# Fixed tables for the order of calls and of engine queues, a tie maximum in PSUM, and a norm by columns, in a fused attention, Fourier and FFN kernel

## Chip, cores and metric

The kernel runs as one program on one core of a Trainium2 chip. The metric is the device time of one execution in microseconds, as the median of several runs. The core's engines each take their instructions in a fixed order: TensorE (PE, with its weight loads as PEld), VectorE (DVE), ScalarE (ACT), GpSimd (POOL) and SyncE (SP), which here only issues DMAs. Between engines the order is kept by semaphores.

## The reference

For 4 batches, 8 heads, 768 tokens and head size 64 the reference computes an attention in which a query sees only keys of its own cluster, then a block that mixes by Fourier transforms, and an FFN.

```
q_assign = argmax(q_n . c_n);  k_assign = argmax(k_n . c_n)      # 16 centroids per head
scores = where(q_assign == k_assign, q k^T / 8, -1e9);  x = softmax(scores) v      # x: 4 x 768 x 512
mixed = real(fft(fft(x, axis=1), axis=2));  u = x + mixed
un = (u - mean(u)) / sqrt(var(u) + 1e-6)
out = u + relu(un @ w_ch1) @ w_ch2                                # 512 -> 2048 -> 512
```

All of it is to fp32 accuracy. The kernel gets there with products of fp16 halves: a value is scaled by a power of two and split into a high and a low half, and three products (high by high, high by low, low by high) are summed in PSUM.

## The kernel before, in words

Two heads make a pair; there are 16 pairs, 4 to a batch.

`prep(pr)` loads q and k of a pair (one buffer, tag `scr`), takes their largest values and that of v (L492, L524), makes scales, splits q and k into halves (L511, L512), multiplies by the centroids (L539, one PSUM tile `ps_f`), transposes the products into a second `ps_f` tile (L547) and finds the cluster of each token: the maximum over 16 centroids (L553), an equality (L555), a product with tie weights on POOL (L557), the maximum of that (L561, to an SBUF tile `mx`), and three equalities with that maximum (L565 for q, L569 twice for k). The one-hot result is transposed by a DMA.

`scores(pr, st)` makes, for one of six blocks of 128 queries, the score tiles of both heads: 12 matmuls on 64 rows (L596) and 4 mask matmuls on 32 rows (L601) into tiles `ps_big`. Here that is called a score group. For each head follow a scaled maximum on DVE (L615), Exp on ACT (L618), a cast to the high half on ACT (L626), the low half on POOL (L627) and a transposing DMA (L629). `attend` multiplies by v: 18 matmuls for a head and block (L647 to L649), called a product. After each third block `finish` divides by the sums (L659 to L663) into X. `load_v` loads v of a pair; a one-element copy on POOL (L465) from the latest score maximum into the tile ahead of the load ties it to that moment.

`Weights` brings the 32 pieces of the two FFN matrices in through 8 buffers in a scratch region (`arena`) and turns them into fp16 halves: sign bits on ACT (L782, L783), a block maximum (L767, L770), a join (L791, L795) and the halving (L801 to L807).

For a batch whose four pairs are through, `Fourier` folds X (L918, L919), splits and transposes it, and runs the two transforms as matmuls (L977, L993). `FeedForward.norm` gets mean and variance of two tiles of 128 tokens (L1083, L1084), then a power of two near the inverse deviation by five operations on two columns at once (L1085, L1086, L1088, L1090, L1091), applies it on ACT (L1094), splits and transposes. `up` makes 16 hidden blocks of 12 matmuls (L1127, an up group), each with a Relu to fp32 (L1132 or L1134), one to fp16 (L1135) and a difference (L1136); `down` has 8 groups of 12 matmuls (L1157) and two outputs (L1161). A batch has three such blocks of 256 tokens.

PSUM tiles come from three pools: `ps_f` with 3 banks (prep, weights, transforms, FFN), `ps_big` with 2 tiles, `ps_o` with 1.

What runs when is set in two steps. `Overlap.run` gives every call a step of a schedule by constants (T0, STEPS, V, WD, MIX and others), and fills FFN work in by credits; that is the order of the program. `Order` then takes the list of instructions, gives each a cost and its dependencies, plays the engines through in the kernel's own planner (`schedule`) and ties each engine's instructions together in the order that came out:

```
order, self.end = self.schedule()
for xs in order.values():
    for a, b in zip(xs, xs[1:]):
        self.tc.add_manual_dep(self.L[b], self.L[a].name, ...)
```

Of the kernel before, what the change touches and what calls it, by code (L numbers as in the profile page):

```python
# [13 lines left out]
F32 = mybir.dt.float32  # L14
# [42 lines left out]
def top_power(nc, tops, t, s, inv):  # L57

    t = t.bitcast(I32)
    nc.vector.tensor_scalar(out=t, in0=tops.bitcast(I32), scalar1=23, scalar2=None, op0=ALU.logical_shift_right)  # L60
    nc.vector.tensor_scalar(out=t, in0=t, scalar1=-13.0, scalar2=1.0, op0=ALU.add, op1=ALU.max)
    nc.vector.tensor_scalar(out=inv.bitcast(I32), in0=t, scalar1=240.0, scalar2=float(1 << 23), op0=ALU.min, op1=ALU.mult)
    nc.vector.reciprocal(out=s, in_=inv)
# [13 lines left out]
class Order:  # L77
# [6 lines left out]
    LINEAR = {"DVE": (135, 1.0), "Activation": (105, 0.92), "Pool": (160, 1.15)}  # L84
    SMALL = {"DVE": 75, "Pool": 100}
    TWO = {"DVE": 1.17, "Pool": 1.9}
    EXTRA = (
        (lambda e, i, acc: e == "DVE" and len([a for a in acc if a[1]]) > 1, 110),
        (lambda e, i, acc: e == "DVE" and any(a[1] and a[0].startswith("oh_") for a in acc), 310),
        (lambda e, i, acc: e == "Activation" and i.opcode == "TensorCopy", -75),  # L90
        (lambda e, i, acc: e == "Pool" and "pow" in str(getattr(i, "op", "")), 500),
    )
    AFTER = {"DVE": 75, "Activation": 100, "Pool": 40, "PE": 160}
    WAKE = {"DVE": 35, "Activation": 35, "Pool": 78, "PE": 52, "SP": 27}
    COPY, TURN, LAND, RATE = (530, 2150), (960, 0.46), 1790, (0.32, 0.65)
    STRETCH, TURNED = 3413.0, 80
    LATER = ()

    def __init__(self, tc, pools):
        self.tc, self.nc, self.bufs, self.cuts = tc, tc.nc, pools, []  # L100
        self.first = len(self.traced())
# [4 lines left out]
    def cut(self, stream):  # L106
        self.cuts.append((len(self.traced()) - self.first, stream))

    @staticmethod
    def base(name):  # L110
        return name.rstrip("0123456789").rstrip("_")

    def accesses(self, i):

        for w, side in ((0, i.ins), (1, i.outs)):
            for a in side:
                t = getattr(getattr(a, "bass_ap", None), "tensor", None)
                if t is None:
                    continue
                es = {F32: 4, I32: 4, U32: 4, F16: 2, BF16: 2, I16: 2, U16: 2}.get(a.dtype, 4)  # L120
                ap, off = [list(x) for x in a.ap], a.bass_ap.offset
                row = ap[0][0] or 1
                lo = hi = off % row
                n = 1
                for s, c in ap[1:]:
                    n *= c
                    lo, hi = (lo, hi + s * (c - 1)) if s >= 0 else (lo + s * (c - 1), hi)
                yield t.name, w, (off // row, off // row + ap[0][1], lo * es, (hi + 1) * es), n, es

    def cost(self, e, i, acc):  # L130
        n = max([a[3] for a in acc], default=1)
        if e == "PE":
            out, es = [a for a in acc if a[1]][0], [a[4] for a in acc if not a[1]][0]
            share = i.tile_size[0] * i.tile_size[1] / P / P if i.tile_size else 1.0
            return max(out[3] * (4 if es == 4 else 1) / 2.4 + 2.5, 30) * share
        if e == "SP":
            return self.TURN[0] + self.TURN[1] * n if "ranspose" in i.opcode else self.COPY[0]
        a, b = self.LINEAR[e]
        full = [x for x in acc if not x[1] and x[3] * 2 > n and x[3] > 1]
        t = (a if n >= 16 else self.SMALL.get(e, a)) + n * (self.TWO.get(e, b) if len(full) > 1 else b)  # L140
        for test, more in self.EXTRA:
            if test(e, i, acc):
                t += more
        return t

    def pace(self, now, ns):

        at, busy, slow = self.clock
        while now >= at + self.STRETCH:
            share = busy / self.STRETCH  # L150
            slow = share < (0.8 if slow else 0.5)
            at, busy = at + self.STRETCH, max(busy - self.STRETCH, 0.0)
        ns *= 2 if slow else 1
        self.clock = at, busy + ns, slow
        return ns

    def graph(self):
        L = self.L = list(self.traced())[self.first:]
        N = len(L)
        name = lambda i: str(i.engine).split(".")[-1]  # L160
        self.eng = [name(i) for i in L]
        acc = [list(self.accesses(i)) for i in L]
        self.dur = [self.cost(e, i, a) for e, i, a in zip(self.eng, L, acc)]
        self.size = [max([x[3] * x[4] for x in a], default=0) for a in acc]
        deps = [set() for _ in L]
        self.tags = [{self.base(z[0]) for z in a if z[1]} for a in acc]
        tiles, seen, users, hist, before = {}, {}, {}, {}, {}
        self.starts, self.behind = [[] for _ in L], {}
        self.cap, self.held = {}, [[] for _ in L]
        for x, i in enumerate(L):  # L170
            for t, w, r, n, es in acc[x]:
                tag = self.base(t)
                banked = tag.startswith("ps_")
                if t not in seen:
                    seen[t] = x
                    made = tiles.setdefault(tag, [])
                    if made and not banked:
                        self.behind.setdefault(seen[made[-1]], []).append(x)
                    made.append(t)
                    bufs = self.cap[tag] = self.bufs.get(tag, 1)  # L180
                    if banked:
                        self.starts[x].append(tag)
                    elif len(made) > bufs:
                        before[t] = users[made[-1 - bufs]]
                deps[x].update(before.get(t, ()))
                if banked:
                    deps[x].update(y for y in users.get(t, ()) if y != x)
                users.setdefault(t, []).append(x)
                h = hist.setdefault(t, [])
                for y, wy, ry in h:  # L190
                    if (w or wy) and y != x and ry[0] < r[1] and r[0] < ry[1] and ry[2] < r[3] and r[2] < ry[3]:
                        deps[x].add(y)
                if w:
                    h[:] = [z for z in h if not (z[2][0] >= r[0] and z[2][1] <= r[1] and z[2][2] >= r[2] and z[2][3] <= r[3])]
                h.append((x, w, r))
        self.deps = [[y for y in d if not (self.eng[y] == self.eng[x] == "PE")] for x, d in enumerate(deps)]
        self.left = []
        for t, xs in users.items():
            if t.startswith("ps_"):
                xs = set(xs)  # L200
                for x in xs:
                    self.held[x].append(len(self.left))
                self.left.append([self.base(t), len(xs)])
        self.mode = [i.tile_size[0] if e == "PE" and i.tile_size else P for e, i in zip(self.eng, L)]
        self.call, c = [], -1
        for x in range(N):
            while c + 1 < len(self.cuts) and self.cuts[c + 1][0] <= x:
                c += 1
            self.call.append(c)

    def units(self):
        U, last, call = [], None, None
        for x, e in enumerate(self.eng):
            if e == "PE":
                if last != "PE" or any(t != "ps_big" for t in self.starts[x]) or call != self.call[x]:
                    U.append([])
                U[-1].append(x)
                call = self.call[x]
            last = e
        return U  # L220

    def schedule(self):
        eng, dur = self.eng, list(self.dur)
        N, U = len(eng), self.units()
        late = dict(self.LATER)
        rank = [(c + late.get(c, 0), x) for x, c in enumerate(self.call)]
        after = [[] for _ in range(N)]
        wait = [len(d) for d in self.deps]
        for x, d in enumerate(self.deps):
            for y in d:  # L230
                after[y].append(x)
        for xs in self.behind.values():
            for x in xs:
                wait[x] += 1
# [31 lines left out]
        while True:  # L266
# [40 lines left out]
            if not events:  # L307
                break
# [1075 lines left out]
```

## Time and profile before

| what | value |
|---|---|
| median of 3 runs | 1002.15 us (998.67 to 1002.95) |
| profiled execution | 1003.47 us, span 1001.4 us |
| mean granted TensorE clock | 0.956 of full speed |
| PE busy | 896.3 us (90% of the span) |
| PEld busy | 586.1 us (59%) |
| DVE busy | 599.3 us (60%) |
| ACT busy | 604.3 us (60%) |
| POOL busy | 601.6 us (60%) |
| chain that ended last, by engine | PE 62%, DVE 14%, ACT 8%, DMA 6%, issue 5%, POOL 4% |

The span is from the first to the last instruction; the execution has some 2 us around it. A granted clock of 1.00 is 2.4 GHz, and half of that is the lower of its two levels; a mean between them says for which share of a stretch each was granted. A group's mean duration mixes calls that ran alone and calls that had to wait within the instruction. "Idle before, releaser" is what ended an engine's idle time.

### The profile page before, as it was taken

The numbers are of one execution on the slowest core, as the hardware profiler recorded it, in microseconds if no ns is written. First come the engines' busy times: TensorE is split into PE (matmuls) and PEld (weight loads), VectorE is DVE, ScalarE is ACT, GpSimd is POOL, SyncE is SP. The second block draws the span as 40 slices with busy tenths as digits, with TensorE's granted clock in tenths as the row PEclk, the third lists the DMA queues.
The fourth block names the chain that finished last, engine by engine and source line by source line (L and its number), as shares of the span: only waits on it lengthen the run. The fifth ranks groups of instructions, "written<-read, shape, count | busy, mean of one in ns | idle before, by whom it ended". The sixth has DMA issues, their size and how long they took to land.

```text
span 1001.4 us, 23416 instructions
## 1 busy us (share of the span) xinstructions
PE 896.3 (90%) x9349; PEld 586.1 (59%) x9368; DVE 599.3 (60%) x1276; ACT 604.3 (60%) x948; POOL 601.6 (60%) x702
## 2 busy tenths in 40 slices
PE   3775768578899999999999999889999999899998
PEld 1243444356666757666757667556658585576683
DVE  7788979789555655879555646767554335611110
ACT  6899989656756756557656656557656352342130
POOL 2467667667866756759857567559757462552230
PEclk9799877778899999999999999999999999999999
DMA  7799999979768666699676666689765552311000
GB/s 263 196 225 256 267 226 238 198 157 179 143 118 175 108 154 134 123 181 212 116 167 118 154 118 143 122 151 180 118 125 109 107 106 59 71 26 33 11 11 22
DMA packets 397374, 140.65 MB, mean 140 GB/s; under 512 B 381904, under 2 KB 382928, under 8 KB 397264
## 3 DMA queue, kind: packets, MB, share of 16 engines
q1 hardware_dynamic: 397264, 139.16, 67.4%
q8 instruction: 73, 1.20, 0.5%
q14 instruction: 37, 0.30, 0.1%
HBM read 43.17 MB, written 6.29 MB: 49 GB/s over the span
## 4 chain that ended last, share of the span: by engine, by line
PE 62%; DVE 14%; ACT 8%; DMA 6%; issue 5%; POOL 4%; SPq 1%; DVEq 0%; ACTq 0%; POOLq 0%
PE ps_f L1157 21%; PE ps_f L1127 20%; PE ps_big L596 7%; PE ps_f L977 3%; PE ps_o L647 2%; PE ps_o L648 2%; PE ps_o L649 2%; DVE ps_big L615 2%; PE ps_big L601 2%; DMA scr<-in_q_dram 2%; DMA pt<-p 1%; ACT p L618 1%; POOL ph L627 1%; DVE X L615 1%; DMA arena<-in_moe_w_ch_dram 1%
## 5 line engine op out<-in xcount | busy, mean ns | idle before, releaser
L627 POOL TENSOR_TENSOR ph<-p,ph 128x768 f16<-128x768 f32 x144 | 241.3, 1678 | 137.0 <-ACT ph L626 101.0
L1127 PE MATMUL ps_f<-arena,w1h 128*128 128x256 f16 x1536 | 267.1, 274 | 11.3 <-ACT arena L1135 11.2
L1157 PE MATMUL ps_f<-w2h,arena 128*128 128x512 f16 x768 | 239.3, 379 | 0.2 <-ACT arena L1135 0.2
L1127 PE MATMUL ps_f<-arena,w1l 128*128 128x256 f16 x768 | 210.7, 274 | 0.0
L618 ACT ACTIVATE p<-ps_big,rmx 128x768 f32<-128x768 f32 x144 | 128.9, 898 | 129.5 <-DVE ps_big L615 82.2
L615 DVE TENSOR_SCALAR_CACHE_REDUCE ps_big<-ps_big,sce 128x768 f32<-128x768 f32 x144 | 142.0, 1020 | 68.8 <-PE ps_big L601 67.5
L1157 PEld LDWEIGHTS <-arena 128*128 128x128 f16 x1152 | 109.0, 98 | 125.9 <-issue 5.0
L1136 POOL TENSOR_TENSOR arena<-arena 128x256 f16<-128x256 f32 x192 | 130.9, 691 | 79.8 <-ACT arena L1135 75.7
L1127 PEld LDWEIGHTS <-w1h 128*128 128x128 f16 x1536 | 151.0, 98 | 23.2 <-issue 4.8
L596 PE MATMUL ps_big<-hlk,hlq 64*128 64x384 f16 x1152 | 127.2, 345 | 22.6 <-ACT p L618 11.8
L1157 PE MATMUL ps_f<-w2l,arena 128*128 128x512 f16 x384 | 145.5, 379 | 0.0
L626 ACT CAST ph<-p 128x768 f16<-128x768 f32 x144 | 118.9, 828 | 27.2 <-DMA pt<-ph 26.9
L647 PE MATMUL ps_o<-v,pt 128*128 128x66 f16 x1152 | 123.7, 198 | 11.5 <-DMA pt<-p 7.5
L648 PE MATMUL ps_o<-v,pt 128*128 128x64 f16 x1152 | 123.6, 199 | 0.0
L649 PE MATMUL ps_o<-v,pt 128*128 128x66 f16 x1152 | 123.2, 197 | 0.0
L647 PEld LDWEIGHTS <-pt 128*128 128x128 f16 x1152 | 109.7, 100 | 22.2 <-DMA pt<-p 8.3
L1132 DVE TENSOR_SCALAR arena<-ps_f,wrel 128x256 f32<-128x256 f32 x96 | 46.3, 482 | 121.4 <-PE ps_f L1127 83.7
L1135 ACT ACTIVATE arena<-ps_f,wrel 128x256 f16<-128x256 f32 x192 | 89.6, 474 | 42.4 <-DVE arena L1132 41.9
L648 PEld LDWEIGHTS <-pt 128*128 128x128 f16 x1152 | 110.1, 100 | 4.6 <-issue 0.8
L649 PEld LDWEIGHTS <-pt 128*128 128x128 f16 x1152 | 110.4, 102 | 0.0
L596 PEld LDWEIGHTS <-hlq 64*128 64x128 f16 x1152 | 54.8, 98 | 81.9 <-issue 55.6
L1127 PEld LDWEIGHTS <-w1l 128*128 128x128 f16 x768 | 75.5, 98 | 21.2 <-issue 12.3
(178 smaller groups left out, 1311.9 us busy)
## 6 DMA issues: line engine op xcount, KB each, us to landing
arena<-in_moe_w_ch_dram SPq DMA_DIRECT2D x32, 512.0 KB, 5.2
scr<-in_q_dram SPq DMA_DIRECT2D x16, 384.0 KB, 3.5
scr<-in_k_dram SPq DMA_DIRECT2D x16, 384.0 KB, 4.3
vst<-in_v_dram SPq DMA_DIRECT2D x16, 384.0 KB, 4.0
out_dram<-arena SPq DMA_DIRECT2D x24, 256.0 KB, 2.2
pt<-ph SPq DMA_TRANSPOSE x168, 3.8
arena<-in_cs_dram SPq DMA_DIRECT2D x12, 192.0 KB, 3.9
arena<-in_ss_dram SPq DMA_DIRECT2D x12, 192.0 KB, 3.9
```

Source lines behind the costliest of these rows:

```text
L596: nc.tensor.matmul(out=ps[j][:, hf, 0:SH], lhsT=hq[rows[j], a, sl], rhs=hk[rows[j], c, hs], start=(i == 0), stop=False)
L615: self.mark = nc.vector.tensor_scalar(out=ju, in0=ps[j][:, :, 0:SH], scalar1=ne, scalar2=None, op0=ALU.mult, op1=ALU.min, accum_out=m)
L618: nc.scalar.activation(x, ju, AF.Exp, bias=m, scale=-1.0)
L626: nc.scalar.copy(out=ph[:, 0], in_=p32)
L627: nc.gpsimd.tensor_tensor(out=ph[:, 1], in0=p32, in1=ph[:, 0], op=ALU.subtract)
L647: nc.tensor.matmul(out=o[:, at:at + W], lhsT=hi, rhs=v16[:, kt, 0:W], start=(kt == 0), stop=False)
L648: nc.tensor.matmul(out=o[:, at:at + D], lhsT=hi, rhs=v16[:, kt, 66:130], start=False, stop=False)
L649: nc.tensor.matmul(out=o[:, at:at + W], lhsT=lo, rhs=v16[:, kt, 0:W], start=False, stop=(kt == ST - 1))
L1127: nc.tensor.matmul(out=ps.rearrange("p (t x) -> p t x", x=P), lhsT=a[:, dc, fs], rhs=c[:, :, dc], start=(i == 0), stop=(i == 11))
L1135: nc.scalar.activation(hh[:, f], ps, AF.Relu, scale=rel[:, f:f + 1])
L1136: nc.gpsimd.tensor_tensor(out=hl[:, f], in0=r, in1=hh[:, f], op=ALU.subtract)
L1157: nc.tensor.matmul(out=ps, lhsT=a[:, f, ts], rhs=c[:, f], start=(i == 0), stop=(i == 47))
```

## The change

The planner with its costs goes, and so do the constants of the schedule. In their place stand two kinds of tables, written out as text. `Overlap.PLAN` is the order of calls: every word names a stream (p prep, s scores, a attend, v values, l weight loads, w weight conversion, t transform, n norms, f FFN, c centroids) with its pair or batch, and how many steps of it come next. The calls are cut into smaller steps for that. `Order.TABLE` has a line of numbers for each engine, by which that engine's instructions (for PE: groups of matmuls) are taken out of the order of the program. The instructions of one engine are tied together as before.

Three pieces of the computation change too. The maximum over the tie weights goes to unused columns of the transposes' PSUM tile. The norm makes its small operations column by column, and hands the variance on without a copy. The POOL copy ahead of the v load goes. The scratch region is laid out anew: the weights' pieces come in four double buffers, and the scale of a block is written four columns wide for the second matrix.

```
-    LINEAR = {"DVE": (135, 1.0), "Activation": (105, 0.92), "Pool": (160, 1.15)}
...
-    def schedule(self):
...
+    TABLE = {
+        "PE": """
+.5 2 0 -4 3 0 -5 4 1 -2 1 4 -5 2 1 0 1 -8 0 6 1 -2 1 -6 7 3 -7 0 8 -8 8 -9 3 4 -9 8 0 -7 -3 9 2 1 0 -6 -8 7 -4 7 0 -5 6 -3 2
...
+            for word in self.TABLE[e].split():
+                for step in [0] * int(word[1:]) if word[0] == "." else [int(word)]:
+                    at += 1 + step
+                    order.append(at)
+            order = [x for g in order for x in groups[g]]
             for a, b in zip(order, order[1:]):
                 self.tc.add_manual_dep(
...
-        if self.late is not None:
-
-            nc.gpsimd.tensor_copy(out=t[:, 0, 0:1], in_=self.late)
         nc.sync.dma_start(out=t, in_=self.v[b, :, 2 * hp:2 * hp + 2])
...
-        mx2 = sb.tile([P, G], F32, name="mx", tag="mx")
+        mx2 = ps[:, G * NC_:G * NC_ + G]
         nc.vector.tensor_reduce(out=mx2, in_=a, op=ALU.max, axis=AX.X)
...
-    RAW, PN = tuple(4128 * i for i in range(6)) + (29696, 33824), (24768, 40000, 44096)
+    EARLY, SPARE, PIECE = (0, 8224, 20576, 28800), (0, 8224), 4112
...
-        nc.vector.tensor_scalar(out=mv[:, :, 1], in0=mv[:, :, 1], scalar1=1e-6, scalar2=None, op0=ALU.add)
-        nc.vector.tensor_scalar(out=e.bitcast(I32), in0=mv[:, :, 1].bitcast(I32), scalar1=1, scalar2=0x7F800000,
-                                op0=ALU.logical_shift_right, op1=ALU.bitwise_and)
-        nc.vector.tensor_scalar(out=s[:, 0].bitcast(I32), in0=e.bitcast(I32), scalar1=-1.0, scalar2=float(USC << 23),
-                                op0=ALU.mult, op1=ALU.add)
-        nc.vector.scalar_tensor_tensor(out=s[:, 1], in0=mv[:, :, 0], scalar=-1.0, in1=s[:, 0], op0=ALU.mult, op1=ALU.mult)
-        nc.vector.tensor_copy(out=va, in_=mv[:, :, 1])
-        for j in range(2):
+            nc.vector.bn_aggr(out=mv[:, j, 0:2], in_=st)
+            mean, var, e = (mv[:, j, i:i + 1] for i in range(3))
+            nc.vector.tensor_scalar(out=var, in0=var, scalar1=1e-6, scalar2=None, op0=ALU.add)
+            nc.vector.tensor_scalar(out=e.bitcast(I32), in0=var.bitcast(I32), scalar1=1, scalar2=0x7F800000,
+                                    op0=ALU.logical_shift_right, op1=ALU.bitwise_and)
+            nc.vector.tensor_scalar(out=s[:, 0, j:j + 1].bitcast(I32), in0=e.bitcast(I32), scalar1=-1.0, scalar2=float(USC << 23),
+                                    op0=ALU.mult, op1=ALU.add)
+            nc.vector.tensor_scalar(out=s[:, 1, j:j + 1], in0=mean, scalar1=s[:, 0, j:j + 1], scalar2=-1.0, op0=ALU.mult, op1=ALU.mult)
...
+    PLAN = """
+p0*4 v0 p0 c p0 p1 p0 p1 p0 l v0*2 w c l w p0*4 v1 s0 v2 p1*2 s0*2 p1 s0 p1 l*2 p1 v1 w*4 l*3 v3 l*2 w p2 l w p1*2 p2 s0*2
...
+        for word in self.PLAN.split():
+            name, _, n = word.partition("*")
+            if name not in streams:
+                streams[name] = self.make[name[0]](int(name[1:] or 0))
+            for _ in range(int(n or 1)):
+                self.order.cut()
+                next(streams[name])
```

## Rows read from the trace of the kernel before

**Rows 1.** The page, span in 40 slices: PE's busy tenths, the granted clock.

```profile
PE   3775768578899999999999999889999999899998
...
PEclk9799877778899999999999999999999999999999
```

**Rows 2.** Stage table: stretch, length, busy us (and instructions) by engine, clock, DMA, GB/s.

```profile
0.00:50.00 50.00, 25.27 (x162) 10.74 (x164) 36.31 (x93) 35.53 (x46) 17.20 (x49) 0.90 0.75 230
50.00:175.00 125.00, 87.98 (x1131) 52.01 (x1143) 105.09 (x226) 117.86 (x152) 85.29 (x75) 0.86 1.15 242
175.00:247.00 72.00, 52.13 (x657) 34.85 (x659) 62.30 (x133) 45.80 (x67) 48.76 (x46) 0.79 0.91 179
247.00:425.00 178.00, 173.02 (x1917) 115.84 (x1916) 109.33 (x215) 111.88 (x180) 123.02 (x139) 0.98 0.69 136
425.00:625.00 200.00, 198.37 (x2198) 133.83 (x2195) 130.26 (x282) 126.82 (x208) 140.49 (x163) 1.00 0.76 151
625.00:700.00 75.00, 67.71 (x754) 43.96 (x753) 55.99 (x122) 46.29 (x76) 51.90 (x61) 0.95 0.80 151
825.00:1001.40 176.40, 166.76 (x1162) 109.99 (x1159) 45.85 (x94) 48.90 (x106) 56.75 (x92) 1.00 0.14 34
```

**Rows 3.** Timeline of PE about 246.7 us: start, duration, engine, line, operation.

```profile
246.68 0.40 PE L1127 MATMUL ps_f<-arena,w1h 128*128 128x256 f16 x1
```

**Rows 4.** Chain of waits, 170 to 250 us: start, duration, what.

```profile
190.68 4.35 DMA scr<-in_k_dram
...
200.56 3.12 DMA vst<-in_v_dram
```

**Rows 5.** Waits of DVE, first 247 us: us in total, times, longest.

```profile
DVE amx L492 <- DMA scr<-in_q_dram: 7.6, 3, 4.7
```

**Rows 6.** Busy time (and count) of L596, then of L618, up to 246.7 us.

```profile
0.00:246.70 246.70, 50.65 (x384) 21.40 (x384) 0.85 1.00 222
...
0.00:246.70 246.70, 56.42 (x62) 0.85 1.00 222
```

**Rows 7.** Single lines: count, duration in ns least/median/most, first and last start.

```profile
L686 DVE TENSOR_SCALAR sce<-scp x32: 176/191/205, 11.2 to 717.2; 128x1 f32<-128x1 f32 x32
...
L1085 DVE TENSOR_SCALAR mve<-mve x12: 169/568/1577, 234.1 to 873.4; 128x2 f32<-128x2 f32 x12
```

**Rows 8.** Groups by line, DVE, 225 to 247 us: busy us, mean ns, idle before.

```profile
L1090 DVE SCALAR_TENSOR_TENSOR rpow<-mve,rpow 128x2 f32<-128x2 f32 x2 | 2.0, 1010 | 0.0
L1085 DVE TENSOR_SCALAR mve<-mve 128x2 f32<-128x2 f32 x2 | 1.7, 873 | 0.0
...
L1086 DVE TENSOR_SCALAR mve<-mve 128x2 int32<-128x2 int32 x2 | 1.1, 574 | 0.0
...
L1088 DVE TENSOR_SCALAR rpow<-mve 128x2 int32<-128x2 int32 x2 | 0.8, 399 | 0.0
...
L1091 DVE COPY mv<-mve 128x2 f32<-128x2 f32 x2 | 0.3, 155 | 0.0
```

**Rows 9.** Single line L569, as in rows 7.

```profile
L569 DVE TENSOR_TENSOR oh<-ac,mx x32: 243/346/1702, 22.6 to 753.0; 128x96 bf16<-128x96 f32 x32
```

**Rows 10.** Groups by line, DVE, first 247 us.

```profile
L569 DVE TENSOR_TENSOR oh<-ac,mx 128x96 bf16<-128x96 f32 x12 | 6.2, 520 | 0.0
...
L565 DVE TENSOR_TENSOR oh<-ac,mx 128x192 bf16<-128x192 f32 x6 | 3.0, 507 | 0.0
```

**Rows 11.** Waits in SP's DMA queue, whole span.

```profile
SPq L757 <- DVE ps_f L795: 9.6, 4, 6.6
```

**Rows 12.** Chain of waits, whole span: one up group.

```profile
747.64 1.31 PE ps_f L1127 x12
```

**Rows 13.** Timeline of DVE, 694 to 706 us.

```profile
694.61 0.55 DVE L555 TENSOR_TENSOR ac<-ps_f,mx 128x384 f32<-128x384 f32 x1
...
702.64 2.13 DVE L569 TENSOR_TENSOR oh<-ac,mx 128x96 bf16<-128x96 f32 x2
```

**Rows 14.** Waits of PE, from 247 us on.

```profile
PE ps_f L1127 <- ACT arena L1135: 11.2, 6, 4.4
```

More of the change, by code (lines that the diff above doesn't have):

```diff
@@ L104, in traced, with cut @@
         return self.nc.cur_bb.bb.instructions
-    def cut(self, stream):
-        self.cuts.append((len(self.traced()) - self.first, stream))
+    def cut(self):
+        self.cuts.add(len(self.traced()))
     @staticmethod
[L110 to L209, printed above, removed]
@@ L807, in halve, with loads, convert @@
             nc.vector.scalar_tensor_tensor(out=lo, in0=ps, scalar=s, in1=hi, op0=ALU.mult, op1=ALU.subtract)
-    def run(self):
+    def loads(self):
+        for k in range(32):
+            self.load(k)
+            yield
+    def convert(self):
         nc, at = self.nc, self.arena.at
@@ L1136, in up, with norms, layer @@
             nc.gpsimd.tensor_tensor(out=hl[:, f], in0=r, in1=hh[:, f], op=ALU.subtract)
-            yield 1.3
+            yield
+    def norms(self, b):
+        for blk in range(3):
+            m = self.norm(b, blk)
+            yield
+            self.inverse(*m)
+            yield
+    def layer(self, b):
+        for blk in range(3):
+            yield from self.up(blk)
+            yield from self.down(b, blk)
     def down(self, b, blk):
@@ L1223, in fill @@
-    def fill(self, share):
-        if self.hold == self.now:
-            return
-        self.credit += share * self.left / max(self.end - self.now, 1)
-        while self.credit > 0:
-            c = self.step()
-            if not c:
-                self.credit, self.hold = 0.0, self.now
-                return
-            self.credit -= c
-            self.left -= c
-    def step(self):
-        self.order.cut("rest")
-        return next(self.gen, 0.0)
-    def drain(self, keep):
-        while self.left > keep:
-            c = self.step()
-            if c == 0.0:
-                return
-            self.left -= c or 0.0
@@ new lines, with centroids @@
+"""
+    def __init__(self, tc, att, fft, ffn, wts, order):
+        self.att, self.order = att, order
+        self.make = {"p": att.prep, "s": att.scores, "a": att.attend, "v": att.values, "t": fft.transform, "n": ffn.norms,
+                     "f": ffn.layer, "l": lambda _: wts.loads(), "w": lambda _: wts.convert(), "c": self.centroids}
+    def centroids(self, _):
+        self.att.nc.sync.dma_start(out=self.att.X[1][:, 0, 0:D], in_=self.att.cent.rearrange("h c d -> (h c) d"))
+        yield
+        self.att.centroids()
+        yield
+    def run(self):
+        streams = {}
+        self.att.setup()
+        for word in self.PLAN.split():
[5 more added lines that the diff above has]
+                next(streams[name])
+        assert all(next(g, "end") == "end" for g in streams.values())
```

627 lines of the change are left out of this document (260 added, 367 removed).

## The prediction

> **What bounds the kernel now.** I read the 40 slices first, then the stage table, the chain of waits, and last the groups and waits of single lines. The slices show two halves that differ: from slice 12 on PE is full at the full clock, before that it is not [rows 1]. The stage table gives the sizes. PE is busy for 25.3, 88.0 and 52.1 us of the first 50, 125 and 72 us, under a granted clock of 0.90, 0.86 and 0.79; afterwards it loses little [rows 2]. The losses after 247 us are idle time of 5.0, 1.6, 7.3 and 9.7 us in the stretches that begin at 247, 425, 625 and 825, and what a mean clock of 0.98 and 0.95 takes from the first and the third (0.02 x 178 = 3.6, 0.05 x 75 = 3.8): 31 us together. The first FFN group, which makes PE full, starts at 246.68 us [rows 3]. So the time is 246.7 us, then some 724 us of matmuls that fill PE, then 31 us lost.
>
> What holds that first group back is a stage in which ACT and DVE share the load: ACT is busy 117.9 of the 125 us from 50 on (94%), DVE 62.3 of the 72 us from 175 on (87%) [rows 2]. The chain of waits shows how: it runs through the load of k from 190.68 to 195.03 and through that of v from 200.56 to 203.68 [rows 4]. DVE stands in order behind both; three of its waits for q and k in the first 247 us are 7.6 us, the longest 4.7 [rows 5].
>
> **The change, part by part.**
>
> *The same work before the first FFN group.* The plan and the tables are read so: a word "a4*2" is two steps of a call, a number moves to the group that many places past the next one, ".3" is three in place. Ahead of the first "f0" group the table of PE has 32 score groups and 60 attention products, and that of ACT 64 Exp. Before, PE had done 384 / 12 = 32 score groups, and ACT 62 Exp, when the first up group began [rows 6]. What lies ahead of it is the same to two instructions, so neither the matmuls behind it nor the sums per engine change. The orders can only close gaps.
>
> *Norm by columns.* One call drops five DVE operations of two columns (L1085, L1086, L1088, L1090, L1091) for four per column, eight in all. The five are not dear in themselves: L1085 takes between 169 and 1577 ns [rows 7], and in 225 to 247 us two calls cost 2.0 + 1.7 + 1.1 + 0.8 + 0.3 = 5.9 us [rows 8], with POOL at work beside them (48.8 of 72 us [rows 2]). A one-column TENSOR_SCALAR on SBUF never took more than 205 ns, median 191, in 32 calls [rows 7]. Both norm calls stood ahead of the first up group; in the tables of DVE and ACT only the first block's does. I take 5.9 - 8 x 0.19 = 4.4 us off the path. Ends: -4.4, and -1.2 if one column waits as two do (8 operations at 5.9 / 10 = 0.59 are 4.7 us). Later calls lie beside a full PE: nothing.
>
> The Trainium skill (VectorE: DVE Perf Modes, Rules for kernel authors) speaks against this edit: it says that DVE operations should be few, since each pays its own flush. By that alone a call goes from 5 x 0.19 to 8 x 0.19, +0.6 us, and the sum below would be 5 us higher. The spread from 169 to 1577 ns of one and the same instruction is not a flush, so I go by the row.
>
> *Tie weights in PSUM.* The maximum over the tie weights goes to the free columns of the transposes' bank, so the three comparisons of a pair read one operand from PSUM. L569 runs from 243 to 1702 ns [rows 9]; in the first 247 us its 12 calls and the 6 of L565 cost 6.2 and 3.0 us [rows 10]. L569's least is 0.25 us; L565 has 96 elements more, at 1.07 ns each by the step from that least to L555's 0.55 us for 384 [rows 13], so 0.35. With 12 and 6 of these, 5.1, the comparisons lose 4.1 us. Ends 0 and -4.1. The price is that the ps_f bank stays taken until the last comparison; that is the third rival.
>
> *Loads.* The POOL copy that tied each v load to an earlier maximum is gone (L465), and the tables place the DVE reads of p6's loads behind the first fold. I take away the longest wait, 4.7 us [rows 5]; ends 0 (another load is late instead) and -7.6. The weights now move through four double buffers and each load is its own step of the plan; 24 of the 32 wait for a buffer as before. Such waits held SP for 9.6 us in 4 cases, the longest 6.6 [rows 11], with the transposing DMAs queued behind. I take 0; ends -9.6 and 4 x 6.6 - 9.6 = +17. SP's other queue neighbours keep their kind.
>
> *Orders.* What is left idle in the first stage is ACT's 14.5 us before 50 us and DVE's 9.7 - 4.7 = 5.0 after 175 [rows 2]. How much the tables close can't be read off a row; the ends are 0 and the point at which ACT never stops: its 35.5 + 117.9 + 45.8 = 199.2 us of work [rows 2] behind some 3 us of start, that is 202, 45 us earlier than now. I take a third of the 19.5: -6.5. With the other terms ACT is then busy 199.2 / 227 = 88% of the stage, halfway between its 81% now and the 94% of its densest stretch. Together the first up group moves by 4.4 + 4.1 + 4.7 + 6.5 = 20 us, to about 227.
>
> *After it.* The tables lay matmuls between the last attention product of a batch and its first transform group: 3 up and 5 down in batch 1, 5 and 4 in batch 2, 7 and 4 in batch 3, with a few score groups. At 1.31 us an up group and twice that for a down [rows 12], these are at least 17, 17 and 20 us to hide the fold behind. Before, PE stood still or slow for 11 us in 625 to 700. I take 7 of the 31 us away: a quarter, half of that stretch and a little of the first. Ends 0 and -20 (the tail's 3.9 and part of the last stretch stay, since batch 3 has nothing else left to lay between).
>
> **The sum.** The profiled execution took 1003.47 us, 2.1 more than its span. 1003.5 - 20 - 7 = 976.5; the median 1002.15 lies 1.3 lower, so 975. The terms' likely errors (6 us in the first stage, 7 behind it) give 962 to 990 for this case.
>
> **Rivals.** *The orders are nearly tight.* ACT works without a gap, and the first up group starts at 209 instead of 247; the losses behind it fall by 11. 1003.5 - 38 - 11 - 1.3 = 953. For it: ACT reaches 94% already in a stage of 125 us. Against: the chain there changes engine every microsecond, and each change has a gap.
>
> *The orders close nothing.* New gaps come for the old ones, as a fixed order does wherever a DMA lands late; only the 8.5 us of shorter DVE operations stay: 1003.5 - 8.5 - 1.3 = 994. For it: the old order was worked out too, and its waits on ACT and DVE are many and short. Against: the 4.7 us on one load is a plain misplacement.
>
> *The bank that isn't released.* A ps_f bank was free after L555; now it is held until the last L569. For the pair at 694.61 that is from 695.2 to 704.8 us [rows 13], 9.6 us, in which PE has two banks for up groups whose Relus queue behind Exp and casts. PE waited for such a release 6 times after 247 us, 11.2 us, the longest 4.4 [rows 14]. Ten pairs (6 to 15) lie in the FFN stage; at 4.4 us each they cost 44, and the time is 975 + 44 = 1019, slower than before. It decides from 27 / 10 = 2.7 us a pair on. Against: two banks suffice while a Relu pair follows its group at once. The Trainium skill (PSUM — Partial Sum Buffer, Summary) has it that banks are to be emptied promptly; no row here shows a longer hold's price.
>
> *The operations stay long.* One column and one PSUM operand wait like two; the orders still work: 975 + 8.5 = 984.
>
> **Chances.** The forecast 0.45, tight orders 0.20, orders that close nothing 0.15, operations that stay long 0.11, the bank 0.09. A measurement of this kernel tells 0.5%, 5 us, from no change. Forecast, tight and long lie below 997; of the 994 case a bit under half reaches into the band. Faster 0.82, same 0.09, slower 0.09. The range is 949 to 1000: it leaves out the low half of the second case and all of the bank.
>
> **What would show it.** The first up group at 220 to 233 us, and ACT busy over 86% of the time until then. The small norm operations at 0.2 us each and L565 and L569's successors without values over a microsecond; if these still spread, the fourth rival holds. No wait of 4 us of DVE on a q or k load between 180 and 210. PE idle and clock losses of about 24 us behind the first up group. Waits of up groups for ps_f that sum to over 27 us would show the bank and make the prediction wrong; so would a first up group later than 240.

## The result

The changed kernel took 988.85 us in the median of four runs (986.90 to 990.53), the kernel before 1002.32 (998.67 to 1002.95): a ratio of 0.986, 95% interval 0.9845 to 0.9883. The direction was right and the time lay within the range, but of the 27 us forecast 13.5 came: half. That the time lay within the range says little, since the range reached up to 1000; where in the kernel the time was won says more.

The stage table of the changed kernel, with the columns of [rows 2]:

```profile
0.00:50.00 50.00, 23.05 (x189) 10.99 (x193) 36.64 (x94) 35.46 (x48) 18.07 (x48) 0.97 0.79 234
50.00:175.00 125.00, 93.23 (x1153) 54.02 (x1166) 104.93 (x233) 119.17 (x155) 87.49 (x73) 0.84 1.14 248
175.00:247.00 72.00, 50.98 (x629) 34.93 (x631) 61.44 (x133) 44.28 (x68) 46.52 (x43) 0.83 1.00 182
247.00:425.00 178.00, 176.96 (x1976) 118.36 (x1975) 110.58 (x237) 116.01 (x187) 122.68 (x141) 1.00 0.78 144
425.00:625.00 200.00, 194.73 (x2149) 129.97 (x2146) 125.59 (x279) 125.75 (x203) 134.40 (x153) 1.00 0.76 141
625.00:700.00 75.00, 74.30 (x865) 52.83 (x864) 52.65 (x145) 50.85 (x85) 58.34 (x67) 1.00 0.88 166
700.00:825.00 125.00, 120.79 (x1341) 80.73 (x1340) 49.05 (x101) 68.08 (x109) 72.26 (x82) 1.00 0.58 102
825.00:986.60 161.60, 155.70 (x1063) 102.64 (x1061) 38.78 (x97) 45.98 (x99) 51.08 (x85) 1.00 0.15 36
```

Up to 247 us it is the same stage as before: DVE's three entries (the third busy figure of a row) sum to 203.0 us against 203.7 in [rows 2], ACT's (the fourth) to 198.9 against 199.2. Behind it PE's idle time is 1.0 + 5.3 + 0.7 + 4.2 + 5.9 = 17.1 us, at a granted clock of 1.00 throughout, where [rows 2] gave 31 of idle time and clock. (The second profiles of both kernels, e11 and e12 below, give 27 and 19 in the same way.) The first up group (it answers to [rows 3]), in PE's timeline:

```profile
243.85 0.28 PE L1009 MATMUL ps_f<-arena,w1h 128*128 128x256 f16 x1 [1.68 <-DMA arena<-arena]
```

It came 2.8 us sooner, not 20, and so later than 240 us, which the prediction had named as a sign of being wrong. The rest of the gain lies behind it. The busy time up to the first up group, before and after (columns as above):

```profile
0.00:246.68 246.68, 165.07 (x1941) 97.34 (x1961) 203.39 (x450) 198.87 (x264) 150.93 (x168) 0.85 1.00 222
```

```profile
0.00:243.85 243.85, 164.12 (x1942) 97.11 (x1960) 199.87 (x453) 196.80 (x264) 149.09 (x159) 0.86 1.03 226
```

DVE is busy for 3.5 us less and idle for 44.0 us, 43.3 before; ACT is idle for 47.1, 47.8 before. In the first stage the new orders closed no idle time of either engine.

The single operations did what the edits say. DVE by line, first 247 us (they answer to [rows 8, 10]; the columns are busy us and mean ns):

```profile
L796 DVE TENSOR_TENSOR arena<-X 128x1536 f32<-128x1536 f32 x2 | 6.7, 3365 | 0.0
L449 DVE TENSOR_TENSOR oh<-ac,ps_f 128x96 bf16<-128x96 f32 x12 | 2.8, 244 | 0.0
L445 DVE TENSOR_TENSOR oh<-ac,ps_f 128x192 bf16<-128x192 f32 x6 | 2.1, 352 | 0.2
...
L969 DVE TENSOR_SCALAR mv<-mv 128x1 f32<-128x1 f32 x4 | 0.5, 141 | 0.0
L974 DVE TENSOR_SCALAR rpow<-mv,rpow 128x1 f32<-128x1 f32 x2 | 0.4, 209 | 0.0
L972 DVE TENSOR_SCALAR rpow<-mv 128x1 int32<-128x1 int32 x2 | 0.3, 146 | 0.0
L970 DVE TENSOR_SCALAR mv<-mv 128x1 int32<-128x1 int32 x2 | 0.3, 137 | 0.0
```

The comparisons lost 9.2 - 4.9 = 4.3 us, the small operations of norm 5.9 - 1.5 = 4.4. With the splits of v, which fell from 10.6 to 8.2 us, that makes 11.1; but DVE's busy time fell by only 3.5. Others took the rest back: the two folds (L796) cost 6.7 us, 4.8 before, one operation each of L721 and L979 1.2 and 1.1 more, and two more scaled maxima and one more row of norm statistics lay ahead of the first up group. DVE's long wait for q is gone; its longest for a load up to 247 us is 2.2 us, for v. Waits of PE, whole span (us in total, times, longest):

```profile
PE ps_o L535 <- DMA pt<-ph: 23.0, 15, 5.3
...
PE ps_f L1009 <- ACT arena L1017: 2.5, 5, 1.0
```

The second row answers to [rows 14]: 2.5 us where the bank rival needed over 27. The first has grown: PE stands in order on attention products whose transposing DMA has not landed, 14.0 of these 23.0 us between 175 and 247. In the same stretch another wait of PE, that of the scores for Exp, has shrunk from 11.4 to 2.2 us. Waits of PE, 175 to 247 us, before and after:

```profile
PE ps_big L596 <- ACT p L618: 11.4, 6, 3.3
...
PE ps_o L647 <- DMA pt<-ph: 2.2, 2, 1.6
...
PE ps_o L647 <- DMA pt<-p: 1.8, 2, 1.2
```

```profile
PE ps_o L535 <- DMA pt<-ph: 14.0, 6, 5.3
...
PE ps_big L479 <- ACT p L500: 2.2, 3, 1.2
```

New gaps came for old ones.

### The profile page after: what moved, and what is told of

Its sections match the earlier page's. It is cut to its first block, busy times and chain, and to the rows that moved or that the text cites. A ratio compares the mean times of both kernels' runs of the same rounds, so it can differ in the third digit from the quotient of the medians.

```text
span 986.6 us, 23502 instructions
## 1 busy us (share of the span) xinstructions
PE 889.7 (90%) x9350; PEld 584.5 (59%) x9368; DVE 579.7 (59%) x1312; ACT 605.6 (61%) x948; POOL 590.8 (60%) x688
## 5 line engine op out<-in xcount | busy, mean ns | idle before, releaser
L1009 PE MATMUL ps_f<-arena,w1h 128*128 128x256 f16 x1536 | 263.9, 273 | 4.3 <-ACT arena L1017 2.5
L508 ACT CAST ph<-p 128x768 f16<-128x768 f32 x144 | 119.3, 830 | 89.3 <-DMA pt<-ph 88.5
L535 PE MATMUL ps_o<-v,pt 128*128 128x66 f16 x1152 | 127.1, 198 | 33.2 <-DMA pt<-ph 23.0
L479 PE MATMUL ps_big<-hlk,hlq 64*128 64x384 f16 x1152 | 125.1, 342 | 14.2 <-DVE X L498 9.5
L536 PE MATMUL ps_o<-v,pt 128*128 128x64 f16 x1152 | 126.8, 199 | 0.0
L537 PE MATMUL ps_o<-v,pt 128*128 128x66 f16 x1152 | 126.3, 197 | 0.0
```

Of the source, the lines that this page charges most:

```text
L479: nc.tensor.matmul(out=ps[j][:, hf, 0:SH], lhsT=hq[rows[j], a, sl], rhs=hk[rows[j], c, hs], start=(i == 0), stop=False)
L508: nc.scalar.copy(out=ph[:, 0], in_=p32)
L535: nc.tensor.matmul(out=o[:, at:at + W], lhsT=hi, rhs=v16[:, kt, 0:W], start=(kt == 0), stop=False)
L536: nc.tensor.matmul(out=o[:, at:at + D], lhsT=hi, rhs=v16[:, kt, 66:130], start=False, stop=False)
L537: nc.tensor.matmul(out=o[:, at:at + W], lhsT=lo, rhs=v16[:, kt, 0:W], start=False, stop=(kt == ST - 1))
L1009: nc.tensor.matmul(out=ps.rearrange("p (t x) -> p t x", x=P), lhsT=a[:, dc, fs], rhs=c[:, :, dc], start=(i == 0), stop=(i == 11))
```

## The experiments

First up is the start of the first up group in the one profile of each kernel, "behind" the span less that, the time the median of all its runs, the ratio that to the kernel before, measured beside it, with its 95% interval. A profile is one execution and can lie several us off the median of its kernel, so first up and time of a row need not belong together.

| run | first fold | first up | behind | time | ratio |
|---|---|---|---|---|---|
| before | 198.7 | 246.7 | 754.7 | 1002.3 | |
| changed | 188.8 | 243.9 | 742.8 | 988.9 | 0.9864 [0.9845, 0.9883] |
| e11 before again | 198.4 | 246.5 | 752.0 | 1001.8 | 1.0004 [0.9986, 1.0021] |
| e12 changed again | 187.5 | 242.5 | 746.5 | 991.5 | 0.9879 [0.9839, 0.9919] |
| e1 norm and tie, old planner | 191.2 | 243.4 | 750.9 | 992.5 | 0.9910 [0.9887, 0.9932] |
| e15 norm alone | 199.3 | 247.6 | 751.0 | 998.4 | 0.9970 [0.9955, 0.9986] |
| e16 tie alone | 188.9 | 243.5 | 758.6 | 1001.8 | 1.0010 [0.9989, 1.0031] |
| e8 tie in SBUF | 186.9 | 239.8 | 745.8 | 991.0 | 0.9892 [0.9852, 0.9933] |
| e2 norm's chain freed | 190.7 | 244.0 | 744.1 | 988.8 | 0.9863 [0.9837, 0.9888] |
| e3 first fold freed | 191.7 | 247.1 | 742.2 | 990.7 | 0.9889 [0.9868, 0.9910] |
| e4 both | 189.9 | 243.0 | 743.6 | 990.4 | 0.9882 [0.9860, 0.9903] |
| e5 less ACT | 187.8 | 242.4 | 744.1 | 991.0 | 0.9899 [0.9861, 0.9937] |
| e6 less DVE | 186.6 | 240.7 | 742.9 | 986.3 | 0.9848 [0.9811, 0.9885] |
| e7 less DMA | 187.2 | 242.3 | 745.2 | 986.5 | 0.9850 [0.9814, 0.9887] |
| e9 less ACT, DMA | 181.1 | 234.0 | 741.5 | 981.2 | 0.9781 [0.9754, 0.9808] |
| e13 less ACT, DVE | 185.0 | 238.8 | 742.0 | 981.8 | 0.9804 [0.9773, 0.9835] |
| e14 less DMA, DVE | 185.0 | 238.4 | 744.1 | 981.6 | 0.9799 [0.9771, 0.9827] |
| e10 less of all three | 178.6 | 230.2 | 744.0 | 977.0 | 0.9735 [0.9706, 0.9764] |
| e17 more ACT | 199.3 | 253.9 | 743.4 | 999.5 | 0.9971 [0.9956, 0.9987] |
| e18 more DVE | 196.5 | 251.3 | 745.7 | 995.8 | 0.9930 [0.9906, 0.9954] |

**How far one profile can be read** (both kernels again).

> The kernel before once more, for a second profile. If one profile's first up group tells a difference of 3 us: 245.7 to 247.7 again. If first up of the same kernel wanders by several us (the experiments on the changed kernel put its first fold anywhere from 186.6 to 191.7): 242 to 251, and the 2.8 us between before and after is not to be told from none. Time 1000 to 1004.

> The changed kernel once more, for a second profile. By the first reading first up is at 243 to 245 again; by the second at 239 to 247. Time 987 to 991; behind first up 742 to 745.

The first up groups, in PE's timelines of the kernel before and of the changed one:

```profile
246.54 0.28 PE L1127 MATMUL ps_f<-arena,w1h 128*128 128x256 f16 x1 [0.74 <-DMA arena<-arena]
```

```profile
242.48 0.28 PE L1009 MATMUL ps_f<-arena,w1h 128*128 128x256 f16 x1 [1.87 <-DMA arena<-arena]
```

So first up moved from 246.6 to 243.2 (means of two), -3.4, and what lies behind it from 753.4 to 744.6, -8.8. A difference of 2 us in one profile of the changed kernel tells nothing. (e12's "behind" of 746.5 lies outside the 742 to 745 expected.) The eight runs of the changed kernel have their median at 989.9, which is used from here on.

**Arithmetic or tables** (e1, e15, e16 on the kernel before, its planner laying its own orders; e8 on the changed kernel, its tables kept).

```
# e1: both; e15: the norm part; e16: the mx2 line.  e8: the mx2 line the other way
-        mx2 = sb.tile([P, G], F32, name="mx", tag="mx")
+        mx2 = ps[:, G * NC_:G * NC_ + G]
...  # norm: the changed kernel's loop over j in place of the two-column operations
+            nc.vector.tensor_scalar(out=var, in0=var, scalar1=1e-6, scalar2=None, op0=ALU.add)
...
```

> The kernel before with two of the three edits of arithmetic (norm's small operations by columns, the tie comparison's maximum in PSUM) and its own planner, which orders all engines anew; calls and no tables from outside. Theory A (as the forecast priced them): the small operations fall to 0.2 us and the comparisons to 0.25-0.35 us, the first up group comes 8.5 us sooner (near 238), time 994. Rival B (DVE's gain is eaten by other operations of DVE that read two SBUF operands and wait on GpSimd, as in the changed kernel, where DVE's busy time up to 247 did not fall): first up within 2 us of 246.7, time 1000 to 1003, and the tables then hold nearly all of the 13.5 us.

> The kernel before and its planner, with norm's small operations by columns alone. If norm and tie share the 9 us of e1_before_arith as the forecast priced them (4.4 and 4.1): 997. If it is all norm's: 992 to 993. If it is all the tie's: 1001 to 1002.

> The kernel before and its planner, with the tie comparison's maximum in PSUM alone. Shared: 997. All norm's, as e8_tie_in_sbuf suggests (991.0, not to be told from the changed kernel): 1001 to 1002. All the tie's: 992 to 993.

> The changed kernel and its orders, with the tie comparison's maximum back in SBUF. If the forecast's price holds (12 comparisons of 0.52 us instead of 0.25 and 6 of 0.51 instead of 0.35 up to first up, 4.1 us on the path): first up 4 us later, time 993. Rival (they are covered by other waits of VectorE): first up within 1 us, time 987 to 990.

e1 measured 992.5: the kernel before with norm and tie alone has some 9 of the 13 us. What is left, 2.6 to 3.7 us, is that of the tables together with the new scratch layout and the POOL copy that went, none of which was tried apart, and it is hardly clear of the noise. e1's time is that of its theory A, its mechanism is not: first up came 3 us sooner, not 8.5, and is that of the changed kernel:

```profile
243.37 0.39 PE L1124 MATMUL ps_f<-arena,w1h 128*128 128x256 f16 x1
```

The tables show no gain there. Behind it every kernel with the tables has 741.5 to 746.5 us, every one with the planner 750.9 to 758.6; so that is where the tables' share lies (8 us by these profiles, 2.6 by the medians; e1's profiled run was the slowest of its six). One stretch shows a gain of the tables: from 625 to 700 us e1 still loses 75 - 69.0 = 6.0 us at the full clock, the changed kernel 0.7.

```profile
625.00:700.00 75.00, 69.04 (x806) 46.41 (x803) 58.28 (x140) 49.48 (x79) 55.21 (x67) 1.00 0.84 156
700.00:825.00 125.00, 125.00 (x1404) 84.99 (x1401) 50.08 (x112) 72.10 (x117) 76.07 (x81) 1.00 0.63 111
```

The next stretch gives most of that back: e1 loses nothing there, the changed kernel 4.2 us.

The two edits don't add up: norm alone brings 2.8 us, none of it ahead of first up, and tie alone none, since its first up comes 3 us sooner and 5 us are lost behind it. Neither is "shared" nor "all norm's". In e1, e15 and e16 the planner lays every engine's order anew, so they do not tell the worth of a shorter operation from that of another order; norm was not tried by itself under the tables.

In e8 the orders stay, and it does tell. The comparisons cost 11.8 us up to 247 us instead of 4.9 (DVE by line, first 247 us):

```profile
L449 DVE TENSOR_TENSOR oh<-ac,mx 128x96 bf16<-128x96 f32 x12 | 7.9, 672 | 0.0
...
L445 DVE TENSOR_TENSOR oh<-ac,mx 128x192 bf16<-128x192 f32 x6 | 3.9, 656 | 0.2
```

DVE works 6.9 us more in its comparisons, and e8 is not to be told from the changed kernel: 991.0, and a first up of 239.8 that is sooner, not later (its profiled run was the fastest of its four). The interval of the time, 4 us to either side, could hide the 4.1 us of the tie edit by itself; first up, no later with 6.9 us more of DVE ahead of it, speaks against them.

**Theory A: single waits in order hold the first stage** (e2, e3, e4; two such waits were tried). In the changed kernel the cast of the norm stood on ACT behind a cast that waited 2.7 us for a transposing DMA, and the first fold ran on DVE beside three operations of POOL. Timelines of DVE and POOL:

```profile
188.78 4.98 DVE L796 TENSOR_TENSOR arena<-X 128x1536 f32<-128x1536 f32 x1
...
201.79 1.75 DVE L796 TENSOR_TENSOR arena<-X 128x1536 f32<-128x1536 f32 x1
```

```profile
188.48 0.96 POOL L808 TENSOR_TENSOR arena<-arena,X 1x255 f32<-1x255 f32 x1 [2.22 <-DVE X L549]
189.41 1.62 POOL L509 TENSOR_TENSOR ph<-p,ph 128x768 f16<-128x768 f32 x1
191.00 1.14 POOL L678 TENSOR_TENSOR w2l<-arena,w2h 128x512 f16<-128x512 f32 x1
```

```
# in Order.apply, behind the decoding of a table:
+            for a, z in self.MOVES.get(e, ()):
+                order.insert(z, order.pop(a))
# e2
+    MOVES = {"Activation": [(242, 243), (249, 253)], "Pool": [(144, 146)], "SP": [(137, 139)], "PE": [(167, 169)]}
# e3 (e4: both)
+    MOVES = {"Pool": [(125, 122)], "Activation": [(217, 215)], "DVE": [(316, 313)], "SP": [(115, 114)],
+             "PE": [(133, 134), (136, 140), (136, 139), (135, 138)]}
```

> The changed kernel with five items moved in its tables: on ScalarE the cast of call s4 (item 10) stands behind the transform's L923, and the cast of item 12 behind the two casts of the first norm; GpSimd's, SyncE's and TensorE's items that hang on item 12 (lo part, transposing DMA, product) behind the norm's. Theory A (the first up group is held by in-order waits: norm's cast stood behind a cast that waited 2.7 us for a transposing DMA, L923 behind one that waited 2.2): first up at 240 to 241 instead of 243.85, time 985.5 (-3.4). Rival B (what sets the first stage is the work of DVE and ScalarE, and a wait that goes is followed by another): first up within 1 us of 243.85, time 988 to 990.

> The changed kernel with its tables edited around the first fold: GpSimd's second fold operation ahead of the three operations that ran beside DVE's fold (4.98 us; 1.75 alone); the fold's split, ScalarE copy and transposing DMA ahead of amx and of items of s4; on TensorE the three odd groups ahead of the products a4 (items 2 and 3) that waited for their transposing DMAs. Theory A: the fold takes 1.8 to 2 us, the first odd group starts at 200 to 202 instead of 206.7, first up 3 us sooner (near 241), time 985.5 to 986. Rival B: the odd groups come sooner but the even ones, norm and first up do not (DVE and ScalarE have the same work to do before it): first up within 1 us, time 988 to 990.

> Both edits of the tables (those of e2_late_norm and e3_early_fold). Theory A: they add up, first up at 237 to 238, time 982 to 983. Rival B: one of them, or neither, shows in first up, time 985 to 989.

Each edit did its part. In e3 the fold is short, and the first odd group (of the first transform's matmuls, L857 of the changed kernel) follows it by 13.0 us instead of 17.9; DVE's timeline of e3:

```profile
191.72 1.75 DVE L800 TENSOR_TENSOR arena<-X 128x1536 f32<-128x1536 f32 x1
```

But the second fold stands behind scores and maxima, the even groups wait for that one, and first up comes no sooner (247.1). In e2 the norm's cast comes 43.3 us after the fold instead of 46.6, and PE is late in its place, standing on two products (PE's timeline of e2):

```profile
236.66 0.20 PE L539 MATMUL ps_o<-v,pt 128*128 128x66 f16 x1 [2.75 <-DMA pt<-ph]
...
239.86 0.24 PE L539 MATMUL ps_o<-v,pt 128*128 128x66 f16 x1 [2.47 <-DMA pt<-ph]
```

No time was won (988.8, 990.7, 990.4). For these two waits theory A falls: one goes and another ends last. The `ph` tile that a transposing DMA reads has two buffers; a third was not tried, and ACT's 88.5 us of waiting for them over the span (27.7 before) stay unexplained.

**One engine too busy?** (e5, e6, e7: work left out, one resource each.)

```
# e5, in Weights.signs: a quarter of the columns from the fourth pair of blocks on
+        w = DM if n < 3 else DM // 4
...
+            nc.scalar.activation(pn[:, i, :, 0:w].bitcast(I16), x[:, :, 0:w], AF.Relu, ...)
# e6, in Weights.join and Attention.largest
+        x, rest = ps.bitcast(U32)[:, 0:DM // 4], rest[:, 0:DM // 4]
...
+        if i < 2 and pr < 6:
+            x = x[:, 0:S // 4]
# e7, in Weights.load
+        w = 4 * DM if k < 8 else 2 * DM
...
```

> The changed kernel, all orders kept; left out: from the fourth pair of weight blocks on, three quarters of the columns of the two ScalarE operations that take the weights' signs (26 operations of 1.22 us become about 0.39, as 257-wide ones took; 21.6 us of ScalarE's work before the first fold). Theory A (ScalarE's work, 119 of 125 us busy in 50 to 175, sets the first stage): the first fold (188.8) and first up (243.85) come 10 to 20 us sooner, and the time falls by about as much, to 970-979. Theory B (VectorE's work sets it) and C (the DMA engines, 9 tenths busy or more in nearly every slice of 50 to 175, set it): first up within 3 us, time 986 to 990.

> The changed kernel, all orders kept; left out: three quarters of the columns of VectorE's 32 weight joins (0.69 us each) and of amx for q and k of pairs 0 to 5 (12 of 0.94), by the 128-wide and 192-wide rows some 22 us of VectorE's work before the first fold, as much as e5_less_scalar takes from ScalarE. Theory B (VectorE's work sets the first stage, as the forecast had it): first up 10 to 20 us sooner, time 970 to 979. A and C: first up within 3 us, time 986 to 990.

> The changed kernel, all orders kept; left out: half the columns of 24 of the 32 weight loads (6.3 MB; 25 us at the 248 GB/s of 50 to 175). Theory C (the DMA engines set the first stage, through the transposing DMAs that stand behind loads): products a3 and a4 stop waiting, first fold and first up 10 us or more sooner, time below 980. A and B: first up at most 3 us sooner (the waits of the products were covered), time 985 to 990.

None of the three theories holds by itself: first up comes 0.8, 2.5 and 0.9 us sooner than 243.2, and the times of e6 and e7, 3.6 and 3.4 us below 989.9, are hardly clear of the noise. In e5 the quarter-width operation took 0.52 us, not 0.39, so 26 x 0.70 = 18 us of ACT went; in e6 20 us of DVE. The stretch from 50 us on, of e5, of e7 and of e9:

```profile
50.00:175.00 125.00, 89.88 (x1147) 51.57 (x1159) 104.67 (x235) 105.13 (x155) 87.02 (x73) 0.86 1.15 248
```

```profile
50.00:175.00 125.00, 90.88 (x1165) 52.70 (x1178) 105.01 (x241) 120.18 (x156) 89.40 (x75) 0.88 0.99 203
```

```profile
50.00:175.00 125.00, 95.27 (x1236) 54.14 (x1235) 110.37 (x253) 108.24 (x160) 92.16 (x78) 0.88 1.06 212
```

In e5 ACT does 14 us less in the same time, the DMA engines are as full as before (1.15), and PE waits longer for transposed products (13.6 us between 50 and 188 against 6.9). In e7 the DMA engines have room (0.99) and ACT is full (120.2 of 125). Of these three only e9, where both are relieved, gets more done in the stretch: PE 1236 matmuls and DVE 253 operations, where the changed kernel had 1153 and 233.

**Two or three at once** (e9, e13, e14, e10: the same edits together).

> The changed kernel, all orders kept; left out at once what e5_less_scalar left out (about 21.6 us of ScalarE's work) and what e7_less_dma left out (6.3 MB of loads). Theory D (two resources hold the stretch 50 to 175 together: without ScalarE's 14 us of that stretch the DMA engines were busy in every slice and the products waited for their transposing DMAs 13.6 us instead of 6.9; without the loads ScalarE was busy 120 of 125 us; so each relief alone fell to the other): first fold at 175 to 180, first up at 230 to 236, time 975 to 980. Theory E (no resource: the orders of the tables and the latency of the chain score, max, exp, cast, lo, transposing DMA, product pace the stretch): first up 241 to 243, time 985 to 990.

> The changed kernel, all orders kept; left out what e5_less_scalar and e6_less_vector left out (22 us each of ScalarE's and VectorE's work), the loads whole. Theory D (ScalarE and the DMA engines hold the stretch 50 to 175 together): the DMA engines still hold it, first up at 239 to 241.5, not below 238; time 984 to 987. Theory F (any two reliefs open the stretch): first up near 234 as in e9_scalar_and_dma, time 978 to 982.

> The changed kernel, all orders kept; left out what e7_less_dma and e6_less_vector left out (6.3 MB of loads, 22 us of VectorE's work), ScalarE's work whole. Theory D: ScalarE still holds it, first up at 239 to 241.5, time 984 to 987. Theory F: first up near 234, time 978 to 982.

> As e9_scalar_and_dma, and VectorE's relief of e6_less_vector (22 us) too. Theory D: first up 3 to 6 us sooner than in e9_scalar_and_dma and the time with it, 970 to 977. Theory E: first up 238 to 242, time 983 to 989. If the time follows first up one to one, what lies behind it (742.7 us in the changed kernel) stays within 2 us.

First up in e9 and e10, PE's timelines:

```profile
234.03 0.28 PE L1011 MATMUL ps_f<-arena,w1h 128*128 128x256 f16 x1 [1.08 <-DMA arena<-arena]
```

```profile
230.20 0.28 PE L1013 MATMUL ps_f<-arena,w1h 128*128 128x256 f16 x1 [1.49 <-DMA arena<-arena]
```

e9's first up comes 9.2 us sooner, e5's and e7's together 1.7. By the position of first up theory D is nearer: e13 and e14 stay at 238.8 and 238.4. By the time theory F is right: 981.8 and 981.6, as e9's 981.2. The profiles mislead here: e9's was its fastest run, 3.9 us below its median, e14's its slowest, 2.7 above. The times go by all runs, and by them the three pairs are not to be told apart.

Settled is that two give 8 us where one gives 0 to 3.6, three 12.9, and that theory E (pace by orders and latency alone) is wrong. Not every pair gives more than its parts: loads and DVE give 3.6 + 3.4 = 7.0 us one by one and 8.3 together, which is the same within the noise. With ACT it is otherwise: 2.5 us one by one and 8.1 together with DVE, 2.3 and 8.7 together with the loads. So it is the work taken from ACT that pays only when another limit goes too. Behind first up the four lie within 2.6 us of each other in their profiles.

**Work added** (e17, e18).

```
# e17, in Weights.signs                      # e18, in Attention.largest, pairs 0 to 5
+        nc.scalar.activation(pn.bitcast(I16), twice, ...)   # out 2048 wide, the second half written again next
...
+            x = x.rearrange("p (o s) -> p o s", o=1).broadcast_to([P, 2, S])
```

> The changed kernel, all orders kept; 16 of ScalarE's sign operations made twice as long (2048 wide instead of 1024; the second half is written over by the next operation): by the 1.22 us of the row and the 0.39 of a 257-wide one some 18 us more of ScalarE's work before the first fold. If ScalarE, busy 119 of 125 us in 50 to 175, is at its bound there: first up and the time 12 to 18 us later (1002 to 1008). If the stretch is paced by latency and orders, with room on every engine: less than 4 us (990 to 994).

> The changed kernel, all orders kept; amx of pairs 0 to 5 (18 operations of 0.94 us) read twice over, by a stride of zero: some 15 us more of VectorE's work before the first fold. If an operation of VectorE is on the path there, as the forecast had it when it took norm, tie and load wait off at one to one: 10 to 15 us later (1000 to 1005). If VectorE has room (20 of 125 us idle in 50 to 175): 2 to 6 us (992 to 996), and ScalarE's 18 us in e17_more_scalar cost more than these.

The lengthened operations, ACT by line in e17 and DVE by line in e18 (busy us, mean ns):

```profile
L639 ACT ACTIVATE arena<-arena 128x2048 int16<-128x2048 int16 x16 | 34.4, 2148 | 1.4 <-PE ps_f L666 1.4
```

```profile
L376 DVE TENSOR_REDUCE amx<-scr 128x1 f32<-128x1536 f32 x12 | 20.6, 1744 | 1.0 <-DMA scr<-in_q_dram 1.0
...
L376 DVE TENSOR_REDUCE amx<-vst 128x1 f32<-128x1536 f32 x6 | 10.5, 1746 | 0.8 <-DMA vst<-in_v_dram 0.8
```

ACT got 16 x 0.93 = 14.9 us more and the time rose by 9.6 (0.64 a microsecond); DVE 18 x 0.80 = 14.4 more, and it rose by 5.9 (0.41). Taking 18 us from ACT gave nothing, 20 from DVE 3.6 (0.18). e17's 999.5 lies between its two expectations, e18's 995.8 in that of a DVE that has room. Adding is dearer than taking away is worth, on either engine. That ACT is near its bound (121.6 us of the 125 from 50 on in e17) fits this and the pairs above; that DVE's share of the cost comes from the same cause is argued, not shown.

## Why the forecast was half right

**The step that failed:** "Together the first up group moves by 4.4 + 4.1 + 4.7 + 6.5 = 20 us, to about 227." It moved by 3.4. Term by term the single operations did what was forecast (4.4 and 4.3 us less for norm and tie, the 4.7-us wait for a load gone), but they were counted one to one as time of the stage, and they are not. DVE's busy time up to first up fell by 3.5 us instead of 8.5, and it is not the measure either: e6 takes 20 us of DVE out of that stage and first up comes 2.5 us sooner; e8 puts 6.9 us of comparisons back and first up comes no later. The prediction had the evidence in [rows 2] and named it, ACT busy for 94% from 50 us on beside DMA engines at 1.15, and then took three of the four terms off DVE's path alone. The second rival's "only the 8.5 us of shorter DVE operations stay" counted them in the same way.

**Orders, -6.5, and load wait, -4.7, in the first stage:** no gain shows. DVE's and ACT's idle time up to first up is what it was (44.0 and 47.1 us), and e1 has the same first up without the tables. The wait for k, on the chain of [rows 4], went away, the first fold came 10 us sooner (188.8 against 198.7), the first odd group 6.7 us and the first up group 2.8: the gain was given back on the way, by the timelines to transposing DMAs, to scores that stand before the second fold, and to POOL beside DVE. ACT's share of the time until first up should have been over 86%; it is 196.8 / 243.85 = 81%, as before.

**Later norm calls, nothing:** norm alone (e15) brings 2.8 us and none of it ahead of first up, where the prediction had put its 4.4. Whether the later calls bring it or the order that the planner laid anew was not tried.

**After it, -7:** right in size, -8.8 by the two pairs of profiles, and in part in its mechanism. The losses went from 31 to 17 us (27 to 19 in the second pair); the 625 to 700 stretch lost 11 us and now loses 0.7, at full clock. Of these 11 the kernel e1, without the tables, still loses 6.0: that part went with the tables, as forecast, though 4.2 us of idle time came up in the stretch behind it, where e1 has none. The clock's part is gone in e1 too, so it is not theirs alone.

**Rivals:** the bank held longer is refuted by 2.5 us of waits, operations that stay long by the rows of L449 and L969. "Orders close nothing", at 994 with a chance of 0.15, was nearest in its mechanism: new gaps came for the old ones. It was rated low because of one misplaced load, which was real; its wait went, and at first up nothing of that is seen.

## What to carry to other kernels

Before a microsecond of an engine's time is taken as a microsecond of the stage, set the busy time of all engines and of the DMA engines side by side for that stretch. Here ACT stood at 95%, DVE at 84% and the DMA engines at 1.14 from 50 us on: shortening ACT or DVE alone was paid at a fifth or less, and lengthening one cost 0.41 to 0.64 of what was added. Try two at once before an engine is called free, and lengthen an operation as well as shortening it: adding work needs no new order, and in this kernel its cost stood clear of the noise where the gain of taking work away hardly did. Orders that remove a visible wait should be judged at the last event of the stage (here the first up group), not at the next one.

## What the runs showed of the hardware

A DVE operation with two SBUF operands took 1.75 us alone and 4.98 beside 3.7 us of POOL operations on SBUF, and 1.75 again when e3 moved these away. The Trainium skill (SBUF — State Buffer, Who interferes with whom) has it that such an operation contends with GpSimd's reads, and that one with at most one SBUF input, outside the two-port modes, does not. The fold agrees, as do the comparisons: 208 to 251 ns in 32 calls with one operand in PSUM, 225 to 1697 with the maximum back in SBUF under the same orders (e8), 243 to 1702 before [rows 9].

The norm's small operations spread only with two columns: L1085, with one SBUF input, took 169 to 1577 ns [rows 7], its one-column successor L969 123 to 155 in 24 calls. What makes the difference no run here shows.

An ACT operation of int16 at a quarter of the width took 0.52 us against 1.22, not the 0.39 that e5 had expected from 257-wide operations: a price from another form of operation was off by a third.
